# S4D convolution and gated GLU on one core: the last step's v from SBUF to SBUF, its Fourier stage ahead of two more down blocks, the last bank's skip weights on VectorE

## The chip, the cores and the metric

The kernel runs on one core of a Trainium2 chip. The metric is the device time of one execution in microseconds, the median of several executions. A core has a matrix engine (TensorE, PE in the profile), a vector engine (VectorE, DVE), a scalar engine (ScalarE, ACT), a general engine (GpSimd, POOL) and SyncE (SP), which does nothing here but issue DMAs. Each engine works through its own instructions in order. SBUF is the on-chip memory of 128 partitions, PSUM the accumulators that PE writes. 16 DMA engines move data between SBUF and device memory (DRAM) or from SBUF to SBUF. An engine that issues a DMA spends some time on the issue alone; the data lands later.

## The reference

One sequence of 2048 rows and 448 columns is normalised. On it go a long convolution (S4D: 448 channels, a kernel from 256 complex modes for each, convolved by FFT, and a skip term) and a gated unit with 1792 hidden columns. Both are added to the input.

```python
x = A_u                                   # [1, 2048, 448]
xn = _layernorm(x, axis=-1)
# A: S4D convolution
dt = exp(log_dt); A = -exp(log_A_real) + 1j * A_imag
C = (C_real + 1j * C_imag) * dt[:, None]
P = exp((A * dt[:, None])[:, :, None] * pos[None, None, :])
K = 2.0 * einsum("dn,dnl->dl", C, P).real
y = irfft(rfft(xn.T, 2 * L) * rfft(K, 2 * L), 2 * L)[:, :, :L].T
yA = y + xn * D_skip
# B: gated unit
h = sigmoid(xn @ w_gate) * (xn @ w_up)
yB = h @ w_down
return x + yA + yB
```

## The kernel before

Two streams of work are interleaved by weights: `glu()` (B) and the convolution's (A). Each is a Python generator that yields how much PE work it has just written; the driver lets the stream that is behind write next. The tile scheduler then orders the instructions of each engine by what is ready, with two helps in the code: `with hp(HP)` gives instructions a high priority, and `tc.issue_after(ins)` keeps instructions behind a given one. What was written together mostly stays together, and each engine runs its list in order.

**The convolution.** Its kernels K are built 8 channels at a time, in 56 chunks (`NCK`); four chunks fill one PSUM bank `ko` (L615), 14 banks in all. When a bank is closed (`cn % 4 == 3`), ACT copies it to SBUF (`ks<-ko`, L625), POOL adds the skip weights `dm` to its first column (`ks[:, :, 0]`, 128x8, L626), and PE runs the first Fourier stage on it (`first_stage`, into PSUM `kp` and `kq`, L565). ACT copies the result to `sk` and writes it to the DRAM tensor `sk_d`. For the last bank `first_stage` is written with high priority, at once.

Then `spectra()` goes through 17 steps `(h, k)`: half `h` of the columns and four frequency rows from `k` on. `loads` fetches a table, a part of `sk_d` (`skl`) and a part of the transformed input. `there` takes the second Fourier stage of both on PE (`sp`), copies one by ACT (`kc`) and multiplies them on DVE (`yy`, `pd`, L912 to L915). `back` takes the first inverse stage on PE (`pv`, L928), ACT copies it to SBUF (`vt`, 128x4x224, L934), and SP writes `vt` to the DRAM tensor `v_d` (L944). `turned` reads it back turned round (L950): `v_d`'s 448 KB land in 16 of the 128 partitions of `vp`, every eighth from `k // 4` on. Within `vt` partition 4w + q holds, for the four rows i of the step, what belongs to partition 32q + 8i + k/4 of `vp`, at place w. When all eight steps of a half are in `vp`, `last(h, m)` takes the last inverse stage on PE (pv from `wf` and `vp`, L961: 64 matmuls for the two calls m, m + 2) and DVE adds the result to the sums (L969): for m = 0 and 2 to `ac` (the first 1024 rows), for m = 4 and 6 to `accs[2]` and `accs[3]` (`acc` in the profile).

**The gated unit.** It takes the rows in two halves of two tiles of 512 rows. Each tile goes through gate and up matmuls (`gu`, in three passes with high and low parts of the operands), the gate on ACT and DVE (`th`, `hf` L719, `hh`, `hl` L726) and down blocks: 128 rows each, 9 matmuls into `po` (L824) and an add to `acc` on DVE (L829). In the second half some weights are loaded raw and split by POOL into `wh` (a cast, L768) and `wl` (the remainder, L769). The very last group of the unit is called `final`. For its second tile (t = 1) there are four down blocks b = 0 to 3, and the end of the program is there: the calls `lasts[0](1, m)` of the convolution's last stage are written between these blocks, and `out` (L239) writes finished rows to the output, on SP and ACT in turn.

Two more things are near these places: `bk`, a table of 128x2x128, is loaded by POOL at the start of `spectra`, and `ac` is filled from `acc_d` by four SP loads during the steps.

Of the kernel before, what the change touches and what calls it, by code (L numbers as in the profile page):

```python
# [36 lines left out]
HP = 300  # L37
# [94 lines left out]
def s4d_glu_kernel(ctx, tc, io):  # L132
# [327 lines left out]
    def kgen(pk):  # L460
# [124 lines left out]
        for g in range(NCK // NCH):  # L585
            for c in range(NCH):
                cn = g * NCH + c
                S = nxt
                me, mf = (m[:, 2 * DC * (c % 2) : 2 * DC * (c % 2) + 2 * DC] for m in mags)
                if 0 < c < 7 and NCH * (g + 1) < NCK:  # L590
                    with tc.issue_after(fts[0].ins):
                        powers(pms, g + 1, PWS[c], sins[0])
                if cn + 1 < NCK:
                    nxt = ahead(cn + 1)
                    if c % 2 == 1:
                        squares(coming[0])
                yield WK / 2
                Et = tl[f"Et{cn % 2}"]
                Ft = tl["Ft"]
                two = lambda ap: ap.unsqueeze(1).to_broadcast([128, 2, 2 * DC, 32])  # L600
                v.tensor_tensor(Et[:, :, :, 32:64], two(me[:, :, 32:64]), S[:, 1::-1], ALU.mult)  # L601
                v.tensor_tensor(Et[:, :, :, 0:32], two(me[:, :, 0:32]), S[:, 1:3, :, ::-1], ALU.mult)  # L602
                fts[:] = [v.tensor_tensor(Ft, two(mf), S[:, 3:5], ALU.mult)]  # L603
                if cn + 2 < NCK and c % 2 == 0:
                    coming = magnitudes(cn // 2 + 1)
                if c % 2 == 1:
                    mags = coming
                if cn % 4 == 0:
                    ko = psc[-1].tile([128, 8, 64], F32, name="ko", bufs=1)
                for q in range(2):  # L610
                    sl = 2 * (cn % 4) + q
                    for k in range(4):
                        h, cc = k // 2, k % 2
                        for j in range(4):
                            mm = nc.tensor.matmul(  # L615
                                ko[32 * j : 32 * j + 32, sl],
                                Ft[:, cc, DC * h + 4 * q + j],
                                Et[:, cc, DC * h + 4 * q + j],
                                start=(k == 0),
                                stop=(k == 3),  # L620
                                skip_group_check=True,
                            )
                if cn % 4 == 3:
                    ks = tl["ks"]
                    nc.scalar.copy(ks, ko)  # L625
                    nc.gpsimd.tensor_tensor(ks[:, :, 0], ks[:, :, 0], dm[:, cn // 4], ALU.add)  # L626
                yield WK / 2
                if cn % 4 == 2 and cn > 3 or cn + 1 == NCK:

                    with hp(HP) if cn + 1 == NCK else tc.issue_after(glu_mm[0].ins):  # L630
                        first_stage((cn - 3) // 4 if cn + 1 < NCK else cn // 4)
# [97 lines left out]
    def glu():  # L729
        for half in range(2):  # L730
# [4 lines left out]
            for fs_ in ORDER[half]:  # L735
# [68 lines left out]
                for t in range(2):  # L804
                    acc = accs[2 * half + t]
                    for b in range(4):
                        if final and (t, b) == (0, 1):

                            yield None
                        if final and t == 1 and b >= 2:  # L810

                            sp_mm[:] = glu_mm
                            for m in (4 * b - 8, 4 * b - 6):
                                lasts[0](1, m)
                            if b == 3:
                                out(accs[2], 8, 4, slice(H, D), (nc.sync, nc.scalar))
                                out(accs[3], 12, 3, slice(0, D), (nc.sync, nc.scalar))
                        po = psg.tile([128, D], F32, name="po", tag="gu", bufs=4)
                        bs = slice(128 * b, 128 * b + 128)
                        n = 0  # L820
                        with tc.issue_after(sp_mm[0].ins) if glu_on else nullcontext():
                            for (hh, hl), (dh, dl) in zip(hs[t], wts):
                                for a_, w_ in ((hh, dh), (hh, dl), (hl, dh)):
                                    glu_mm[:] = [nc.tensor.matmul(  # L824
                                        po, a_[:, bs], w_, start=(n == 0), stop=(n == 3 * fc - 1)
                                    )]
                                    n += 1
                        with hp(HP):
                            v.scalar_tensor_tensor(  # L829
                                acc[:, b], po, 0.5, acc[:, b], ALU.mult, ALU.add  # L830
                            )
                        yield 0.6 * fc
                        if cross and (t, b) in downs:
                            step(*downs[t, b])
                    if cross:
                        nc.sync.dma_start(acc_d[:, 4 * t : 4 * t + 4], acc)
                    if final and t == 0:
                        out(acc, 8, 4, slice(0, H), (nc.gpsimd,))
                    elif final:
                        out(acc, 15, 1, slice(0, D), (nc.sync, nc.scalar))  # L840

    def spectra(pf):
# [76 lines left out]
        def back(h, k, ys_):  # L919
            vt = work("vt", [128, 4, H], 2)  # L920
            bt, n = (t32[:, 1:3], 1) if k == 32 else (bk, 2)
            pvs = [bank("pv") for _ in range(n)]
            with after():
                for j in range(2):
                    for e in range(2):
                        for i in range(n):
                            s = slice(64 * i, 64 * i + 64)
                            mm = nc.tensor.matmul(  # L928
                                pvs[i][:, j], bt[s, e], ys_[j][s, e], start=(e == 0), stop=(e == 1),
                                skip_group_check=True,  # L930
                            )
            sp_mm[:] = [mm]
            for i in range(n):
                nc.scalar.copy(vt[:, i::2], pvs[i])  # L934


            if k == 32:
                for j in range(2):
                    nc.sync.dma_start(v_d[j, 0, 1::2, 0], vt[0:128:2, 2 * j])
            elif k == 0:  # L940
                nc.sync.dma_start(v_d[h, 0, 0::2], vt[0:128:2])
                nc.sync.dma_start(v_d[h, 0, 1::2, 1:4], vt[1:128:2, 1:4])
            else:
                nc.sync.dma_start(v_d[h, k // 4], vt)  # L944

# [65 lines left out]
            yield WS  # L1011
        sp_mm[:] = glu_mm
        back(*prev)
        for t in (*wait, prev[:2]):
            turned(*t)

    def conv():
# [136 lines left out]
```

## Time and profile before

| | |
|---|---|
| time, median of 3 runs (lowest, highest) | 715.69 us (715.16, 718.53) |
| the profiled execution's own time | 711.65 us |
| its span in the trace | 709.9 us |
| mean granted clock of PE | 0.984 |
| last matmul ends | 703.2 us |
| last add of DVE (L829) | 703.20 to 703.82 us |

The page gives one execution, taken by the hardware profiler. "Span" is the time from the first to the last instruction or landing; the execution's own time has 1.75 us more. Times in the views count from the start of the span. The chain that ended last is followed back from the last instruction: at each step to whatever released it, so a change in what is on the chain can move the end, and a change beside it moves the end only if it becomes late enough to join. "PEldq", "SPq" and "ACTq" are the engines' sequencers, which issue DMAs and wait at semaphores. Rows of groups read: line, engine, operation, output<-input, count, then the shortest, median and longest duration in ns, and when the first and the last began. Rows of single instructions begin with the start and the duration in us. Rows of windows give, for a stretch of time, the busy us of PE, PE's weight loads, DVE, ACT and POOL with the count of instructions, PE's granted clock, the DMA engines' mean share and the GB/s moved.

### The profile page before, as it was taken

Reading aid. Unit: us, or ns where it says so; the run is one execution under the profiler, and the core shown is the slowest. Engines: PE = TensorE matmul, PEld = TensorE weight load, DVE = VectorE, ACT = ScalarE, POOL = GpSimd, SP = SyncE. Lnnn points to the kernel's source line nnn. Section 1 sums busy time; section 2 is a strip of 40 time slices with the busy share of each in tenths; the row PEclk is TensorE's granted clock in tenths of the full one; section 3 lists DMA queues with packets and bytes.
Section 4 is the critical chain, followed back from the end, with each engine's and each line's share of the span. In section 5 each row is a group of like instructions: output and inputs, shape, how many; then the busy total and the mean of one; then the engine's idle time right before and its main releaser. Section 6 shows DMA issues by size and latency. Waiting matters only on the chain.

```text
span 709.9 us, 19096 instructions
## 1 busy us (share of the span) xinstructions
PE 669.7 (94%) x7752; PEld 526.9 (74%) x7752; DVE 559.8 (79%) x766; ACT 428.8 (60%) x678; POOL 386.4 (54%) x433
## 2 busy tenths in 40 slices
PE   2797999999998998999999999999989999999996
PEld 2575888778877885756878878877777777777784
DVE  5899997689999999898489899988947555565544
ACT  3655975488698779987577778778543322322320
POOL 2100137645999979896447798798755001335001
PEclk9998999999999999989999999999999999999999
DMA  9947174364244435546933333142259988899756
GB/s 199 245 145 227 52 210 160 130 209 139 69 154 155 150 81 162 186 132 203 283 103 103 92 112 112 64 146 74 56 169 284 250 236 237 222 292 251 182 151 181
DMA packets 93031, 117.22 MB, mean 165 GB/s; under 512 B 12240, under 2 KB 76624, under 8 KB 92944
## 3 DMA queue, kind: packets, MB, share of 16 engines
q1 hardware_dynamic: 65376, 91.75, 45.8%
q10 hardware_dynamic: 24896, 18.13, 8.8%
q0 software_dynamic: 2672, 6.13, 3.2%
q8 instruction: 61, 1.00, 0.6%
q14 instruction: 26, 0.21, 0.1%
HBM read 72.13 MB, written 43.84 MB: 163 GB/s over the span
## 4 chain that ended last, share of the span: by engine, by line
PE 68%; DVE 11%; DMA 7%; ACT 4%; SPq 3%; POOL 3%; issue 2%; ACTq 0%; DVEq 0%; POOLq 0%
PE gu L708 28%; PE po L824 15%; PE sp L901 7%; PE ko L615 6%; PE pv L928 4%; PE tr L541 4%; SPq L491 2%; DVE Ft L603 2%; POOL me L519 1%; DMA wraw<-in_B_w_gate_dram 1%; DVE Et L602 1%; PE pv L961 1%; DMA xe<-in_A_u_dram 1%; DVE Et L601 1%; DMA ph<-ph_d 1%
## 5 line engine op out<-in xcount | busy, mean ns | idle before, releaser
L519 POOL TENSOR_TENSOR me<-me,pm 128x32 f32<-128x32 f32 (+1 forms) x168 | 148.0, 881 | 61.5 <-DVE Et L602 34.1
L519 POOL TENSOR_TENSOR mf<-mf,pm 128x64 f32<-128x64 f32 (+1 forms) x112 | 121.3, 1083 | 5.3
L708 PE MATMUL gu<-xh,wh 128*128 128x512 f32 x336 | 100.7, 406 | 1.7 <-DVE acc L829 0.9
L708 PE MATMUL gu<-xh,wl 128*128 128x512 f32 x336 | 96.6, 391 | 0.0
L708 PE MATMUL gu<-xl,wh 128*128 128x512 f32 x336 | 95.5, 391 | 0.0
L824 PE MATMUL po<-dh,hh 128*128 128x448 f32 x224 | 85.2, 381 | 5.2 <-DVE hf L719 4.6
L601 DVE TENSOR_TENSOR Et<-me,S 128x1024 f32<-128x1024 f32 x56 | 81.8, 1462 | 10.4 <-ACT S L550 8.8
L547 ACT ACTIVATE S<-tr 128x1024 f32<-128x1024 f32 x56 | 57.8, 1032 | 47.6 <-PE tr L541 42.2
L603 DVE TENSOR_TENSOR Ft<-mf,S 128x1024 f32<-128x1024 f32 x56 | 82.3, 1469 | 4.4 <-PE ko L615 2.3
L602 DVE TENSOR_TENSOR Et<-me,S 128x1024 f32<-128x1024 f32 x56 | 81.2, 1449 | 5.0 <-ACT me L532 4.6
L824 PE MATMUL po<-dl,hh 128*128 128x448 f32 x224 | 83.3, 372 | 0.0
L824 PE MATMUL po<-dh,hl 128*128 128x448 f32 x224 | 82.0, 370 | 0.0
L724 ACT CAST hh<-hf 128x512 fp32r<-128x512 f32 x56 | 34.9, 624 | 71.8 <-DVE hf L719 66.8
L708 PEld LDWEIGHTS gu<-xh,wh 128*128 128x128 f32 x336 | 61.2, 191 | 21.6 <-issue 4.6
L708 PEld LDWEIGHTS gu<-xh,wl 128*128 128x128 f32 x336 | 62.9, 188 | 14.5 <-DVE ve L255 0.7
L615 PEld LDWEIGHTS ko<-Et,Ft 128*32 128x32 f32 x3584 | 55.4, 112 | 24.2 <-issue 12.3
L708 PEld LDWEIGHTS gu<-xl,wh 128*128 128x128 f32 x336 | 62.9, 188 | 13.5
L615 PE MATMUL ko<-Et,Ft 128*32 128x64 f32 x3584 | 66.2, 225 | 3.5 <-DVE Ft L603 3.3
L785 POOL TENSOR_TENSOR dl<-rd,dh 128x448 fp32r<-128x448 f32 x14 | 26.2, 1868 | 77.3 <-ACT dh L784 40.0
L550 ACT ACTIVATE S<-S,hpi 128x1024 f32<-128x1024 f32 x56 | 65.7, 1173 | 0.0
L719 DVE SCALAR_TENSOR_TENSOR hf<-th,gu 128x512 f32<-128x512 f32 x56 | 38.0, 679 | 34.3 <-PE gu L708 33.6
L726 DVE TENSOR_TENSOR hl<-hf,hh 128x512 fp32r<-128x512 f32 x56 | 46.7, 833 | 18.6 <-ACT hh L724 14.1
(208 smaller groups left out, 1310.7 us busy)
## 6 DMA issues: line engine op xcount, KB each, us to landing
sk_d<-sk ACTq DMA_DIRECT2D x14, 512.0 KB
sx<-x_d SPq DMA_DIRECT2D x32, 224.0 KB
skl<-sk_d SPq DMA_DIRECT2D x16, 448.0 KB
vp<-v_d SPq DMA_DIRECT2D x16, 448.0 KB
v_d<-vt SPq DMA_DIRECT2D x14, 448.0 KB
ph<-ph_d SPq DMA_DIRECT2D x224, 24.0 KB
wt_d<-wh SPq DMA_DIRECT2D x9, 512.0 KB
wt_d<-wl SPq DMA_DIRECT2D x9, 512.0 KB
```

Source lines behind the costliest of these rows:

```text
L519: ins = nc.gpsimd.tensor_tensor(m[:, :, w + a : 2 * w : n], m[:, :, a:w:n], par(base + i).unsqueeze(2).to_broadcast([128, 4 * DC, w // n]) ...
L547: nc.scalar.activation(rows(cs), pv, AF.Abs)
L550: sins[:] = [nc.scalar.activation(cs, cs, AF.Sin, scale=-TWO_PI, bias=hpi)]
L601: v.tensor_tensor(Et[:, :, :, 32:64], two(me[:, :, 32:64]), S[:, 1::-1], ALU.mult)
L602: v.tensor_tensor(Et[:, :, :, 0:32], two(me[:, :, 0:32]), S[:, 1:3, :, ::-1], ALU.mult)
L603: fts[:] = [v.tensor_tensor(Ft, two(mf), S[:, 3:5], ALU.mult)]
L615: mm = nc.tensor.matmul(ko[32 * j : 32 * j + 32, sl], Ft[:, cc, DC * h + 4 * q + j], Et[:, cc, DC * h + 4 * q + j], start=(k == 0), stop=( ...
L708: glu_mm[:] = [nc.tensor.matmul(ps, a_, b_, start=(n == 0), stop=(n == len(mm) - 1))]
L719: marks[1] = v.scalar_tensor_tensor(hf, th, 1.0, pgu[1], ALU.add, ALU.mult)
L726: v.tensor_tensor(hl, hf, hh, ALU.subtract)
L824: glu_mm[:] = [nc.tensor.matmul(po, a_[:, bs], w_, start=(n == 0), stop=(n == 3 * fc - 1))]
L901: mm = nc.tensor.matmul(to, tb[:kk, t, 64 * c : 64 * c + 64], rhs, start=True, stop=True, skip_group_check=True,)
```

## The change

Three things. For the last bank of the convolution's kernels (chunk 55), ACT copies all columns but the first, and DVE writes the first column: `ks[:, :, 0] = ko[:, :, 0] + dm`, with PSUM as one input. For the last step, (1, 28), `vt` isn't written to `v_d` and read back; 16 DMAs write it from SBUF to SBUF into `vp`, one for each of the 16 partitions of `vp`, each of 28 KB from 32 partitions of `vt`, in turn on SP, ACT, SP, ACT, POOL. And the two pairs of last-stage calls stand ahead of the down blocks b = 1 and b = 3 of the last tile, where they stood ahead of b = 2 and b = 3.

```diff
--- before.py
+++ after.py
@@ -622,8 +622,13 @@
                             )
                 if cn % 4 == 3:
                     ks = tl["ks"]
-                    nc.scalar.copy(ks, ko)
-                    nc.gpsimd.tensor_tensor(ks[:, :, 0], ks[:, :, 0], dm[:, cn // 4], ALU.add)
+                    if cn + 1 < NCK:
+                        nc.scalar.copy(ks, ko)
+                        nc.gpsimd.tensor_tensor(ks[:, :, 0], ks[:, :, 0], dm[:, cn // 4], ALU.add)
+                    else:
+                        with hp(HP):
+                            nc.scalar.copy(ks[:, :, 1:], ko[:, :, 1:])
+                            v.tensor_tensor(ks[:, :, 0], ko[:, :, 0], dm[:, cn // 4], ALU.add)
                 yield WK / 2
                 if cn % 4 == 2 and cn > 3 or cn + 1 == NCK:
 
@@ -807,10 +812,10 @@
                         if final and (t, b) == (0, 1):
 
                             yield None
-                        if final and t == 1 and b >= 2:
+                        if final and t == 1 and b in (1, 3):
 
                             sp_mm[:] = glu_mm
-                            for m in (4 * b - 8, 4 * b - 6):
+                            for m in (2 * b - 2, 2 * b):
                                 lasts[0](1, m)
                             if b == 3:
                                 out(accs[2], 8, 4, slice(H, D), (nc.sync, nc.scalar))
@@ -940,6 +945,12 @@
             elif k == 0:
                 nc.sync.dma_start(v_d[h, 0, 0::2], vt[0:128:2])
                 nc.sync.dma_start(v_d[h, 0, 1::2, 1:4], vt[1:128:2, 1:4])
+            elif (h, k) == steps[-1]:
+                engs = (nc.sync, nc.scalar, nc.sync, nc.scalar, nc.gpsimd)
+                for n in range(16):
+                    q, i = n % 4, n // 4
+                    p = 32 * q + 8 * i + k // 4
+                    engs[n % 5].dma_start(vp[h][p : p + 1], vt[q::4, i])
             else:
                 nc.sync.dma_start(v_d[h, k // 4], vt)
 
@@ -1011,7 +1022,7 @@
             yield WS
         sp_mm[:] = glu_mm
         back(*prev)
-        for t in (*wait, prev[:2]):
+        for t in wait:
             turned(*t)
 
     def conv():
```

How this moves the instructions is seen in each engine's list. DVE around the last bank, before; rows give the line, the operation, output<-input and the shape, and `yy` is the first product of the convolution's steps (the weight split `wl` of POOL isn't on this engine):

```order
L719 SCALAR_TENSOR_TENSOR hf<-th,gu 128x512
L726 TENSOR_TENSOR hl<-hf,hh 128x512
L719 SCALAR_TENSOR_TENSOR hf<-th,gu 128x512
L726 TENSOR_TENSOR hl<-hf,hh 128x512
L912 TENSOR_TENSOR yy<-kc,sp 128x448
```

And of the changed kernel, whose lines below the first edit count 5 more:

```order
L724 SCALAR_TENSOR_TENSOR hf<-th,gu 128x512
L731 TENSOR_TENSOR hl<-hf,hh 128x512
L631 TENSOR_TENSOR ks<-ko,dm 128x8
L724 SCALAR_TENSOR_TENSOR hf<-th,gu 128x512
L731 TENSOR_TENSOR hl<-hf,hh 128x512
L917 TENSOR_TENSOR yy<-kc,sp 128x448
```

The new add stands behind one `hl` of the gated unit and ahead of the next `hf`; everything else keeps its place.

DVE at the end of the program, before (`acc<-po,acc` is a down block's add, `ac<-ac,pv` and `acc<-acc,pv` are the last stage's):

```order
L915 TENSOR_TENSOR yy<-pd 128x224
L829 SCALAR_TENSOR_TENSOR acc<-po,acc 128x448 x6
L969 TENSOR_TENSOR ac<-ac,pv 128x2x224 x4
L829 SCALAR_TENSOR_TENSOR acc<-po,acc 128x448
L969 TENSOR_TENSOR acc<-acc,pv 128x2x224 x4
L829 SCALAR_TENSOR_TENSOR acc<-po,acc 128x448
```

and of the changed kernel:

```order
L920 TENSOR_TENSOR yy<-pd 128x224
L834 SCALAR_TENSOR_TENSOR acc<-po,acc 128x448 x5
L980 TENSOR_TENSOR ac<-ac,pv 128x2x224 x4
L834 SCALAR_TENSOR_TENSOR acc<-po,acc 128x448 x2
L980 TENSOR_TENSOR acc<-acc,pv 128x2x224 x4
L834 SCALAR_TENSOR_TENSOR acc<-po,acc 128x448
```

The first pair of last-stage calls moves one down block earlier, and the second keeps its place ahead of the last block; the matmuls on PE move in the same way.

SP's DMAs at the end, before (`out_dram` is the output; the two pairs of `v_d` and `vp` are those of the steps (1, 24) and (1, 28)):

```order
L944 DMA v_d<-vt 128x896
L950 DMA vp<-v_d 16x32x224
L944 DMA v_d<-vt 128x896
L950 DMA vp<-v_d 16x32x224
L239 DMA out_dram<-ac 32x4x224 x4
L239 DMA out_dram<-acc 32x4x224 x2
```

and of the changed kernel:

```order
L955 DMA v_d<-vt 128x896
L961 DMA vp<-v_d 16x32x224
L953 DMA vp<-vt 1x32x224 x7
L239 DMA out_dram<-ac 32x4x224 x4
L239 DMA out_dram<-acc 32x4x224 x2
```

SP's last write of `v_d` and last read of `vp` are gone, and 7 of the 16 direct DMAs stand there. ACT has 6 more of them, behind its two copies to `vt` and ahead of its outputs, and POOL 3, ahead of its outputs of the rows that the first tile finished. In the program the DMAs of SP and ACT take turns at eight counters that tell of their landing, and one that takes a counter again waits for the earlier one to land. So SP's last three of the seven wait for the landing of three of the first five of the 16, ACT's fourth for the landing of the `vp` read of step (1, 24), and ACT's last two for the first and the fourth of the 16. Elsewhere POOL loads `bk` ahead of the cast to `dh` that it stood behind, and SP's fourth load of `ac` stands ahead of a load of `skl` that it stood behind.

## The prediction

> **What bounds the kernel now.** I read the page first, then the chain that ended last, then PE's waits, then the two places that the change touches.
>
> ```profile
> span 709.9 us, 19096 instructions
> ...
> PE 68%; DVE 11%; DMA 7%; ACT 4%; SPq 3%; POOL 3%; issue 2%; ACTq 0%; DVEq 0%; POOLq 0%
> ```
>
> The chain runs on PE for 68% of the span. From 526 us to the last matmul PE's waits (view of waits, 526 to 712 us) have one entry, which is the wait that ends there:
>
> ```profile
> PE kp L565 <- POOL ks L626: 1.8, 1, 1.8
> ```
>
> So from 526 us on PE works without a pause that another engine ends, and whatever shifts PE there shifts the end by as much. The pieces of the chain at both places:
>
> ```profile
> 524.37 0.03 issue
> 524.40 0.90 POOL wh L768
> 525.30 0.11 issue
> 525.40 0.66 POOL ks L626
> 526.06 0.04 issue
> 526.10 0.27 PE kp L565
> ...
> 686.30 9.49 PE po L824 x45
> 695.79 1.67 PE pv L961 x64
> 697.46 2.01 PE po L824 x9
> ...
> 703.20 0.62 DVE acc L829
> ```
>
> PE stands still from 524.37 to 526.10, since the skip weights' add waits behind POOL's cast of a weight tile. At the end PE goes from one down block (po, 9 matmuls, 2.01 us) to the last Fourier stage (pv) and back; what follows the last add of 703.20 is output DMA. The change can win at three places at most: those 1.73 us, PE's work at the end (which stays the same), and the tail from 703.82 to 709.9.
>
> **VectorE adds the last bank's skip weights.** Removed: one POOL add (0.66 us, in the chain). Added: one DVE add of 128x8. The ACT copy ahead of it stays, with 63 of 64 columns.
>
> ```profile
> 524.63 0.58 ACT L625 COPY ks<-ko 128x512 f32<-128x512 f32 x1
> 524.76 1.22 DVE L726 TENSOR_TENSOR hl<-hf,hh 128x512 fp32r<-128x512 f32 x1 [0.69 <-ACT hh L724]
> 526.02 2.37 POOL L769 TENSOR_TENSOR wl<-wraw,wh 128x1024 fp32r<-128x1024 f32 x1
> L258 DVE TENSOR_TENSOR z<-ys x9: 149/161/166, 9.8 to 72.1; 128x4 f32<-128x4 f32 x6, 128x8 f32<-128x8 f32 x3
> ```
>
> The new add stands behind hl on DVE, and hl ends at 524.76 + 1.22 = 525.98: it takes 1.22 us in place of the usual 0.69, because POOL's cast (524.40 to 525.30) is in its way. So the add runs from 525.98 for 0.16 us (the 128x8 row of L258), and with the 0.04 us of the chain from one engine to the next kp starts at 526.18, where it starts at 526.10 today. The cover of the removed POOL add was hl all along: **+0.1 us, not a gain**. If the cast came after hl, hl would end at 525.45 and kp could start at 525.65: -0.45 is the lower bound. The upper one: with its add gone, POOL's wl stands straight behind the cast. If wl went ahead of hl, hl and the add behind it would wait for 2.37 us. The nearest rows, from 545 us, show the same pair cast and wl with DVE work beside it:
>
> ```profile
> 546.39 0.54 DVE L915 TENSOR_TENSOR yy<-pd 64x224 f32<-64x224 f32 x1
> 546.86 0.60 DVE L913 TENSOR_TENSOR pd<-kc,sp 64x448 f32<-64x448 f32 x1
> 547.39 2.03 DVE L914 TENSOR_TENSOR yy<-yy 64x224 f32<-64x224 f32 x1
> 545.46 1.23 POOL L768 CAST wh<-wraw 128x1024 fp32r<-128x1024 f32 x1 [6.69 <-DMA wraw<-in_B_w_up_dram]
> 546.77 2.40 POOL L769 TENSOR_TENSOR wl<-wraw,wh 128x1024 fp32r<-128x1024 f32 x1
> ```
>
> L915, asked for during the cast, came through at 546.93, ahead of wl's reading; L914, asked for after wl had begun, took 2.03 us in place of 0.38. hl is in the place of L915, so I take the good order. L913, which reads PSUM and one SBUF tile as the new add does, took its usual 0.60 beside wl. The Trainium skill's page "SBUF — State Buffer", section "Who interferes with whom", says it as a rule: a DVE instruction with two SBUF inputs contends with a GpSimd instruction that reads SBUF, one with at most one SBUF input doesn't. The trace agrees with it at L914 and L913; were the new add stopped by wl, the sum would be 2.3 us higher.
>
> On POOL the load of bk moves from behind the dh cast to ahead of it. dl, and the five weight loads behind it, then start about 0.5 us earlier (the length of that issue), so the cast of 545.46 may meet L914's first run at 545.41. PE takes its pv there off this DVE work, so up to +0.5 us, or nothing; the loads land when the DMA engines let them, and I take 0. On SP the fourth ac load goes ahead of one skl load, which is wanted a whole step later: 0.
>
> **The last stage moves ahead of block 1.** No PE work is added: the first pair of last steps starts one po block (a fifth of the chain's 9.49 us for 45 matmuls, 1.90 us) earlier than 695.72, at 693.8, and the second pair stays. What it needs is vp, and today vp is only just there:
>
> ```profile
> 695.72 1.74 PE L961 MATMUL pv<-vp,wf 64*32 64x224 f32 x64
> L961 PEldq EVENT_SEMAPHORE x9: 51/51/3042, 629.7 to 692.1; - x9
> 685.32 0.54 SPq L950 DMA_DIRECT2D vp<-v_d  x1
> 687.32 0.32 SPq L944 DMA_DIRECT2D v_d<-vt  x1
> 690.68 0.54 SPq L950 DMA_DIRECT2D vp<-v_d  x1
> ```
>
> PE's sequencer stood at this wait from 692.1 for 3.04 us, to 695.1, 0.6 us ahead of its use. With the old route the moved stage would wait 1.3 us. The new route must land 1.3 us earlier.
>
> **v from SBUF to SBUF.** Removed: the write of 687.32, the 3.36 us that SP waits for it, and the read of 690.68. Added: 16 DMAs of 28 KB, each from 32 partitions into one: 7 on SP, 6 on ACT, 3 on POOL. In the new order SP's last three and ACT's last two wait, each, for an earlier one of the same 16 to land (ACT's fourth for the vp load of 685.32), so there are two waves.
>
> ```profile
> 686.33 0.97 ACT L934 COPY vt<-pv 128x448 f32<-128x448 f32 x2 [3.89 <-PE pv L928]
> L239 ACTq DMA_DIRECT2D out_dram<-ac x4: 376/470/897, 698.5 to 700.0; - x4
> DMA to landing us min/median/max: 2.3/4.7/6.5
> 686.00:687.00 1.00, 1.00 (x8) 0.72 (x5) 0.00 (x0) 0.67 (x2) 0.00 (x0) 1.00 0.26 40
> 687.00:688.00 1.00, 1.00 (x7) 0.91 (x6) 0.00 (x0) 0.29 (x1) 0.00 (x0) 1.00 0.95 271
> 688.00:689.00 1.00, 1.00 (x6) 0.92 (x5) 0.61 (x1) 0.00 (x0) 0.00 (x0) 1.00 1.24 244
> ```
>
> The first wave is issued from 687.3 on: four on SP at 0.32 (row of v_d), three on ACT at 0.47. It queues behind the vp load of 685.32, as the write does today, and if it lands as that write does, it is there 3.36 us later, at 690.7. The second wave lands 2.3 us (the quickest of the POOL outputs, in the row of landings) to 3.36 us after that: 693.0 to 694.1, so PE waits 0 to 0.3 us; I take 0.1. POOL's three (0.55 us an issue) land within 2.3 to 4.7 us of some 688.9, by 693.6 at the latest. Behind these issues nothing stands on SP and ACT before the outputs of ac, and on POOL only outputs. This estimate holds if 28 KB into **one** partition go as fast as into many; that no row shows, and it is the far bound:
>
> ```profile
> 692.00:694.30 2.30, 2.30 (x13) 2.09 (x12) 0.96 (x2) 0.00 (x0) 1.27 (x3) 1.00 1.00 227
> 305.00:305.50 0.50, 0.50 (x46) 0.50 (x35) 0.50 (x2) 0.50 (x2) 0.42 (x2) 1.00 1.07 418
> ```
>
> The vp load fills 16 partitions at 227 GB/s with all DMA engines busy (share 1.00); a load into all 128 ran at 418. So the rate hangs on how many partitions are written at once: 14.2 GB/s each at 16. If a partition takes no more than that, one DMA needs 28.7 KB / 14.2 = 2.02 us. With all 16 side by side that is no loss; with one DMA for each of the three queues at a time it is 16 / 3 x 2.02 = 10.8 us.
>
> **The tail.** The outputs of ac are issued 1.9 us earlier and are out of the way when those of acc start at 702.19.
>
> ```profile
> 703.00:704.00 1.00, 0.16 (x1) 0.00 (x0) 0.62 (x1) 0.00 (x0) 0.00 (x0) 1.00 0.84 198
> 704.00:705.00 1.00, 0.00 (x0) 0.00 (x0) 0.00 (x0) 0.00 (x0) 0.00 (x0) 1.00 1.06 320
> ```
>
> From 704 on the DMA engines are full with acc's own outputs. Only the slice from 703 can fill better: (320 - 198) / 320 = 0.4 us at most. That slice is also the start of the new transfers, so I take -0.2.
>
> **Sum**: +0.1 + 0.1 - 0.2 = 0.0 us against the profiled execution's 711.65 us (span 709.9 and 1.75 around it). The median of the runs shown is 715.69, 4.0 above it; I put the same sum on it: **715.7 us**. Bounds of the small terms: -0.45 - 0.4 = -0.9 below, +0.5 + 0.3 + 0.1 = +0.9 above.
>
> **Rivals.**
> 1. *One partition at a time is slow* (slower). Data starts at 688.6, when the vp load of 685.32 is through (40 KB by 687, 271 more by 688, and the rest of its 448 KB at 244 GB/s). Then vp is full at 688.6 + 10.8 = 699.4 and PE, which has nothing else in order, waits 5.6 us: 721.3. With two DMAs side by side 16.2 us and a wait of 11.0: 726.7. It costs anything only from the point at which the 16 take longer than 693.8 - 688.6 = 5.2 us, that is with fewer than seven at a time. For it: each DMA writes a single partition, and neighbours in the list are issued together; the 227 against 418. Against it: three queues, and 1.8 KB of each DMA for each engine, little enough to run ahead. The Trainium skill's page "SBUF — State Buffer", section "Door 1: The DMA port swizzle", names such a mechanism: bandwidth goes by how many of 16 ports the partitions reach, with 27.6 GB/s measured for one port. By that page's figure one DMA takes 1.04 us, an estimate, and 16 in a row 16.6 us; the trace's 227 GB/s fits its 8 ports for the vp rows, and no run here shows one port alone.
> 2. *wl goes ahead of hl*: +2.3 us, 718.0.
> 3. *The second wave lands late by more than I think* (one or both of the landings at the 4.7 us median, ready at 695.4 to 696.7): 1.6 to 2.9 us, up to 718.6.
> 4. *The add really gains*, with the better tail: 714.8; faster by over 0.5% would need 3.6 us, more than all pauses the change touches on PE.
>
> **How the numbers follow.** Forecast 0.50; rival 1 0.33 (0.22 near 721, 0.11 near 727); rival 2 0.04; rival 3 0.08; rival 4 0.05. A measurement of this kernel tells some 0.5%, 3.6 us, from no change. Slower by more: rival 1 and little else, 0.34. Faster: 0.03. Same: 0.63. The range runs from 714.5 (the small terms' lower bound, with the runs' own scatter) to 723.0, past the 5.6 us case; it leaves out the 11 us case. The forecast's own range is 714.5 to 717.
>
> **What would show it.** The add right: kp's start, within 0.3 us of 1.8 us after the last ko, released by DVE; hl still at 1.2 us. The route right: no PE wait ahead of the first pv of the last stage, a gap there of 0.3 us as at the others. Rival 1: a gap of several us ahead of that pv, with a high DMA share at few GB/s from 689 us on. The tail right: from the last add to the end 6.0 to 6.1 us, today 703.82 to 709.9. It is wrong if PE waits anywhere else after 526 us, most likely at the pv of 549 us.

## The result and the profile after

| | before | changed |
|---|---|---|
| time, median (lowest, highest) | 715.42 us (714.95, 718.53), 4 runs | 722.12 us (720.94, 725.31), 4 runs |
| ratio, with its 95% interval | | 1.0105 [1.0068, 1.0142] |
| profiled execution's own time, span | 711.65, 709.9 us | 720.94, 719.2 us |
| last matmul ends | 703.2 us | 712.2 us |

The changed kernel is 1.0% slower. Its time lies in the range on record, but not where the forecast had it (715.7 us). PE's waits from 526 us on, in the changed kernel; the columns are us in total, times, longest:

```profile
PE pv L972 <- DMA vp<-vt: 6.1, 1, 6.1
PE kp L565 <- DVE ks L631: 3.2, 1, 3.2
PE pv L972 <- DVE pd L918: 0.2, 1, 0.2
```

Before there was one entry, 1.8 us at kp. Now kp waits 1.4 us longer, and the first last stage waits 6.1 us for the direct DMAs. The chain at the end of the changed kernel (start, us, what) shows them in two waves, and then a slow PE:

```profile
688.33 6.81 DMA vp<-vt
695.14 0.02 issue
695.16 4.59 DMA vp<-vt
699.75 0.52 issue
700.27 3.61 PE pv L972 x61
703.88 4.66 PE po L829 x18
708.54 1.68 PE pv L972 x64
710.21 2.03 PE po L829 x9
```

The DMA of 688.33, the sixth of the 16, takes 6.81 us to land, and the last of the 16, which SP issues only then, 4.59 (SP's last three wait for the second, the third and the sixth). Then the same 64 matmuls that take 1.68 us eight us later take 3.61 (before: 1.67), and the 18 of two down blocks take 4.66 (two times 2.01 before). Windows of the changed kernel, whose last three columns are PE's granted clock, DMA share and GB/s, show what goes with it:

```profile
694.14:698.90 4.76, 0.00 (x0) 0.00 (x0) 0.62 (x1) 0.00 (x0) 1.32 (x3) 0.99 0.54 127
698.90:700.27 1.37, 0.00 (x0) 0.03 (x1) 0.00 (x0) 0.00 (x0) 0.00 (x0) 0.50 0.00 0
700.27:703.88 3.61, 3.61 (x65) 2.30 (x65) 1.15 (x2) 0.00 (x0) 0.00 (x0) 0.50 0.02 5
703.88:708.54 4.66, 4.66 (x26) 4.00 (x33) 1.78 (x3) 0.00 (x0) 0.00 (x0) 0.81 0.60 157
```

After some 4.7 us without a matmul the granted clock falls to 0.50, and stays there into the down blocks. That costs (3.61 - 1.67) + (4.66 - 4.02) = 2.6 us on top of the wait.

The sum for the profiled executions: from the end of the last step's pv (686.30 before, 684.79 + 1.76 = 686.55 now) to the last matmul it is 16.9 us before and 25.7 now. Those 8.8 us are the 6.1 of the wait, the 2.6 of the clock and 0.1. At 686.55 the kernel is only 0.25 us late, since this execution came to kp's place 1.1 us early (PE's wait begins at 526.46 - 3.2 = 523.3 instead of 524.37); from the last add to the end of the span it is 6.3 us instead of 6.1.

The place of kp, in the timelines of DVE and POOL of the changed kernel:

```profile
522.34 0.69 DVE L724 SCALAR_TENSOR_TENSOR hf<-th,gu 128x512 f32<-128x512 f32 x1 [1.13 <-PE gu L713]
523.71 2.61 DVE L731 TENSOR_TENSOR hl<-hf,hh 128x512 fp32r<-128x512 f32 x1 [0.69 <-ACT hh L729]
526.25 0.16 DVE L631 TENSOR_TENSOR ks<-ko,dm 128x8 f32<-128x8 f32 x1
522.32 1.04 POOL L773 CAST wh<-wraw 128x1024 fp32r<-128x1024 f32 x1 [2.57 <-PE gu L713]
523.44 2.33 POOL L774 TENSOR_TENSOR wl<-wraw,wh 128x1024 fp32r<-128x1024 f32 x1
```

POOL's wl begins at 523.44, right behind the cast, and hl, asked for at 523.71, comes through only when wl is done: 2.61 us instead of 0.69. The new add stands behind it.

### The profile page after: what moved, and what is told of

Read it like the earlier page. It is cut to its first block, busy times and chain, and to the rows that moved or that the text cites. A ratio compares the mean times of both kernels' runs of the same rounds, so it can differ in the third digit from the quotient of the medians.

```text
span 719.2 us, 19122 instructions
## 1 busy us (share of the span) xinstructions
PE 671.7 (93%) x7752; PEld 527.6 (73%) x7752; DVE 560.3 (78%) x767; ACT 428.7 (60%) x678; POOL 390.8 (54%) x435
## 4 chain that ended last, share of the span: by engine, by line
PE 73%; DVE 11%; DMA 5%; ACT 4%; SPq 3%; issue 3%; ACTq 0%; DVEq 0%
PE gu L713 31%; PE po L829 15%; PE sp L906 7%; PE ko L615 6%; PE pv L933 4%; PE tr L541 4%; DVE Ft L603 2%; SPq L491 2%; DMA vp<-vt 2%; DVE Et L602 2%; DMA acc<-in_A_u_dram 1%; DVE Et L601 1%; PE pv L972 1%; PE kp L565 1%; DVE m L322 1%
## 5 line engine op out<-in xcount | busy, mean ns | idle before, releaser
L519 POOL TENSOR_TENSOR me<-me,pm 128x32 f32<-128x32 f32 (+1 forms) x168 | 153.4, 913 | 57.4 <-DVE Et L602 29.8
L601 DVE TENSOR_TENSOR Et<-me,S 128x1024 f32<-128x1024 f32 x56 | 80.7, 1443 | 10.2 <-ACT S L550 8.8
L731 DVE TENSOR_TENSOR hl<-hf,hh 128x512 fp32r<-128x512 f32 x56 | 49.8, 890 | 18.6 <-ACT hh L729 14.1
```

The costliest lines, as they stand in the source:

```text
L519: ins = nc.gpsimd.tensor_tensor(m[:, :, w + a : 2 * w : n], m[:, :, a:w:n], par(base + i).unsqueeze(2).to_broadcast([128, 4 * DC, w // n]) ...
L731: v.tensor_tensor(hl, hf, hh, ALU.subtract)
```

## The experiments

Executions of one kernel differ by several us (before: 710.2 to 718.8 over all runs), so two things are read of each run: the ratio with its interval, and, in its one profiled execution, the pieces that the change touches. The table has these for all runs, each from the waits, the chain and the timeline of that kernel; the last column is what the profile's pieces give over before (kp's wait less 1.8, plus pv's end to last matmul less 16.9), beside which the measured ratio can be held (0.1% is 0.7 us). A landing is the one that the chain shows.

| kernel | wait at kp | last v: first issue to last landing | wait ahead of the last stage | end of last back pv to last matmul | ratio [95%] | pieces, us over before |
|---|---|---|---|---|---|---|
| before | 1.8 | 7.8 | 0 | 16.9 | | |
| changed | 3.2 | 12.6 | 6.1 | 25.7 | 1.0105 [1.0068, 1.0142] | +10.2 |
| a1_ks_only | 3.2 | | 0 | 16.9 | 1.0025 [0.9996, 1.0055] | +1.4 |
| a2_move_only | 1.6 | 7.5 | 0.9 | 17.9 | 1.0016 [0.9986, 1.0046] | +0.8 |
| a3_route_only | 1.2 | 10.2 | 1.3 | 18.6 | 1.0046 [1.0016, 1.0076] | +1.1 |
| b2_ports | 3.3 | 10.0 | 2.2 (0.9 and 1.3) | 21.7 | 1.0112 [1.0063, 1.0161] | +6.3 |
| c1_spacer | 1.3 | | 0 | 16.9 | 0.9989 [0.9962, 1.0017] | -0.5 |
| c2_onewave | 1.6 | 8.6 | 1.7 | 19.1 | 1.0056 [1.0030, 1.0081] | +2.0 |
| c3_spread | 3.2 | 8.7 | none waits | 16.8 | one run, 714.01 us | +1.3 |
| c4_no_pool_out | 3.2 | 10.8 | 3.9 | 22.6 | 1.0115 [1.0077, 1.0154] | +7.1 |
| d1_all_mended | 1.3 | 9.5 | 0.8 | 18.2 | 1.0017 [0.9989, 1.0044] | +0.8 |
| d2_after_spacer | 1.3 | 11.2 | 4.4 | 23.9 | 1.0086 [1.0054, 1.0117] | +6.5 |
| d3_after_again | 3.2 | 12.7 | 6.1 | 24.6 | 1.0099 [1.0063, 1.0136] | +9.1 |

Two losses lie outside these pieces: waits of 1.2 and 1.1 us near 651 us in b2_ports and c4_no_pool_out, where a last-stage matmul of the other half waits for VectorE (0.4 us or less in the other kernels), and a low clock behind kp in three profiles, which a1_ks_only shows below.

### The three parts alone

**a1_ks_only**: before with the first part of the diff and nothing else; its core:

```diff
-                    nc.gpsimd.tensor_tensor(ks[:, :, 0], ks[:, :, 0], dm[:, cn // 4], ALU.add)
+                            v.tensor_tensor(ks[:, :, 0], ko[:, :, 0], dm[:, cn // 4], ALU.add)
```

> The kernel before with the VectorE add alone. My theory: the add costs nothing that a measurement can tell; PE's wait at kp is 1.7 to 2.4 us as hl ends when it did, and the time is within 0.5 us of before. Rival: in the changed kernel that wait was 3.2 us in place of 1.8, because hl took 2.61 us beside POOL's wl; if that is what the add brings about, hl takes 2.6 us here too and the time is 1.4 us above before.

PE's wait at kp was 3.2 us. My theory fell. DVE and POOL read as in the changed kernel:

```profile
527.48 2.61 DVE L731 TENSOR_TENSOR hl<-hf,hh 128x512 fp32r<-128x512 f32 x1 [0.68 <-ACT hh L729]
527.20 2.34 POOL L774 TENSOR_TENSOR wl<-wraw,wh 128x1024 fp32r<-128x1024 f32 x1
```

The ratio (1.8 us at its middle) fits the rival's 1.4 us, but its interval just reaches 1. The wait itself is not all. Windows of the wait and of a stretch behind it, and of the changed kernel behind the same wait:

```profile
527.04:530.23 3.19, 0.01 (x2) 0.01 (x1) 2.69 (x2) 0.89 (x2) 2.80 (x3) 1.00 0.12 48
531.68:535.10 3.42, 3.42 (x10) 2.65 (x9) 0.00 (x0) 0.88 (x2) 2.59 (x4) 0.50 0.66 195
526.46:533.28 6.82, 6.82 (x92) 5.50 (x94) 0.36 (x1) 1.73 (x3) 4.73 (x8) 1.00 0.55 156
```

Here PE runs 3.4 us at a granted clock of 0.50 behind the wait of 3.2 us, and so it does in c3_spread and d3_after_again; in the changed kernel, b2_ports and c4_no_pool_out, which waited 3.2 or 3.3 us too, it does not. From kp to the end of the last back's pv the three took 161.6 to 161.8 us, all others 159.8 to 160.9 (without the waits near 651 us), so where the low clock comes it costs about 1 us more.

**a2_move_only**: before with

```diff
-                        if final and t == 1 and b >= 2:
+                        if final and t == 1 and b in (1, 3):
-                            for m in (4 * b - 8, 4 * b - 6):
+                            for m in (2 * b - 2, 2 * b):
```

> The kernel before with the last stage's new place alone; v goes through device memory as before. My theory (the route is at fault, not the place): vp lands at about 695.1 us, the first last stage could start at 693.8, PE waits 1.3 us, and the time is 1.0 to 1.5 us above before. Rival (the place is at fault): 6 to 7 us above before, as in the changed kernel.

The first last stage waited 0.9 us, a little less than expected, with the granted clock at 1.00 throughout. The rival fell: the place alone costs about 1 us in the profile, and by the ratio 3.3 us at most.

**a3_route_only**: before with the last two parts of the diff, the 16 direct DMAs; their core:

```diff
+                    engs[n % 5].dma_start(vp[h][p : p + 1], vt[q::4, i])
-        for t in (*wait, prev[:2]):
+        for t in wait:
```

> The kernel before with the 16 direct DMAs alone, the last stage in its old place. My theory: the last of them lands at 699 to 700 us as in the changed kernel, the first last stage, due at 695.7, waits some 4 us in place of 6, and what PE then runs at a lower granted clock comes on top: 4 to 6 us above before. Rival (the place is at fault): within 0.5 us of before.

Measured 0.46% (3.3 us) over before, a little under what I expected; the wait in the profile was only 1.3 us, not some 4, since the last landing came at 697.2, not 699 to 700. That execution was the fastest of its twelve (713.83 us, median 717.71). Waits and chain of this kernel:

```profile
PE pv L967 <- DMA vp<-vt: 1.3, 1, 1.3
688.25 5.62 DMA vp<-vt
693.87 0.02 issue
693.89 3.32 DMA vp<-vt
697.21 0.03 issue
697.24 2.16 PE pv L967 x62
```

The two waves are there, shorter than in the changed kernel (6.81 and 4.59). After 1.3 us of waiting the clock is still 1.00. In the profiles move and route multiply: the pieces of the three parts alone add up to 3.3 us, those of the changed kernel to 10.2; the old place hides most of the late landing, the earlier place turns it into waiting, and the long wait is followed by the low clock. The times do not show it: by their middles the three parts alone add up to 0.87%, the changed kernel has 1.05%.

### Why wl came ahead of hl

**c1_spacer**: a1_ks_only with one more line behind VectorE's add.

```diff
+                        nc.gpsimd.tensor_tensor(dm[:, 0], ks[:, :, 1], dm[:, 1], ALU.add)
```

> The kernel before with the VectorE add, and one POOL add of 128x8 whose result nobody reads, put where the skip weights' add of POOL stood: it waits for ACT's copy of the bank, as that did, and stands between POOL's cast to wh and wl. Theory (spacer): the old POOL add kept wl from starting until hl was through; without it wl starts 0.08 us behind the cast and holds hl to its end. Then hl takes 0.7 to 1.3 us here and PE's wait at kp is 1.2 to 1.9 us in place of the 3.2 and 3.3 us of the three kernels with the VectorE add, and the time is that of before. Rival (the add's own place on VectorE costs the time): 3.2 us again.

The wait at kp was 1.3 us. DVE and POOL:

```profile
527.94 0.69 DVE L732 TENSOR_TENSOR hl<-hf,hh 128x512 fp32r<-128x512 f32 x1 [0.69 <-ACT hh L730]
528.55 0.16 DVE L631 TENSOR_TENSOR ks<-ko,dm 128x8 f32<-128x8 f32 x1
526.66 1.04 POOL L774 CAST wh<-wraw 128x1024 fp32r<-128x1024 f32 x1 [2.68 <-PE gu L714]
528.47 0.22 POOL L632 TENSOR_TENSOR dm<-ks,dm 128x8 f32<-128x8 f32 x1 [0.78 <-ACT ks L630]
528.66 2.37 POOL L775 TENSOR_TENSOR wl<-wraw,wh 128x1024 fp32r<-128x1024 f32 x1
```

The cast runs beside hf, as in the changed kernel, but POOL then waits 0.78 us for ACT's copy of the bank. In this time hl gets through in 0.69 us, and wl follows. This was what the removed add did unseen: its wait kept wl back. The rival fell. Every profile with VectorE's add and the spacer has 1.3 us at kp, and all but one without it 3.2 or 3.3; the one, c2_onewave, had the cast start 0.86 us behind hf, so that hl was asked for during the cast, as in the profile of before. The time of c1_spacer can't be told from that of before, and 1.3 us at kp is no gain either: with POOL's own add a3_route_only waited 1.2 and a2_move_only 1.6 us.

**d2_after_spacer**: the changed kernel with the same line:

```diff
+                        nc.gpsimd.tensor_tensor(dm[:, 0], ks[:, :, 1], dm[:, 1], ALU.add)
```

> The changed kernel with POOL's spacer add alone. Theory: PE's wait at kp falls from 3.2 us to 1.2 to 1.9, the wait and the low clock ahead of the last stage stay, and the time is 1 to 2 us below the changed kernel's (0.6 to 0.9% above before). Rival (the add is no part of the loss, its wait is made up later): the time of the changed kernel.

The wait at kp fell to 1.3 us as expected, and the wait (4.4 us) and the low clock at the end stayed. The time, 0.86% over before, is on the expected side of d3_after_again's 0.99%, but the intervals overlap: the profile shows the gain, the times don't.

### Why the direct DMAs land late

**b2_ports**: the changed kernel with the 16 in another order.

```diff
-                    q, i = n % 4, n // 4
+                    q, i = (0, 2, 1, 3)[n // 4], n % 4
```

> The changed kernel with the same 16 DMAs on the same queues, in another order of destinations: neighbours in the list now go to partitions 8 apart (7, 15, 23, 31, then 71 and so on) where before they were 32 apart (7, 39, 71, 103, then 15). If the pairs that are 32 apart hold each other up, the first wave lands 1.5 to 3 us earlier, the second with it, PE waits 3 to 4.5 us in place of 6.1, and the time is 1.5 to 4 us below the changed kernel's. If each DMA is slow because it fills one partition only, whichever is beside it, nothing changes: within 1 us of the changed kernel. The Trainium skill's page "SBUF — State Buffer", section "Door 1: The DMA port swizzle", has partitions 32 apart on one port and partitions 8 apart on different ones, and speaks for the first.

The time is that of the changed kernel. The waves took 5.51 and 3.22 us, less than in its profile, but a3_route_only, which has the old order, had 5.62 and 3.32. In both the vp read of step (1, 24), which the first wave queues behind, was issued well ahead of the first direct DMA (2.4 to 2.6 us, by SP's timeline); in the changed kernel only 1.5 us. So held against a3_route_only the order of the destinations made no difference, and how early the read is issued isn't all of it either (in c4_no_pool_out, below, it is 2.9 us ahead and the first wave takes 6.34). But the question stays open. Held against the changed kernel's own two profiles the waves are 1.2 to 1.5 us shorter and the wait is 2.2 us, even less than the first expectation asked; the interval of the ratio leaves room for 2.5 us below the changed kernel; and in the new order neighbours also read the same 32 partitions of vt, where they read different ones. What the Trainium skill's page "SBUF — State Buffer", section "Door 1: The DMA port swizzle", says of partitions 32 apart sharing a port is neither borne out nor refuted by this.

**c4_no_pool_out**: the changed kernel without the line

```diff
-                        out(acc, 8, 4, slice(0, H), (nc.gpsimd,))
```

> The changed kernel without POOL's four outputs of the first tile's rows (rows 1024 to 1535, the first 224 columns are not written), which move 448 KB from 694.5 to 697.5 us, when the second wave lies on the DMA engines. If they hold the second wave up: it lands 2.5 to 3 us after the first in place of 4.6, PE waits 4.0 to 4.6 us in place of 6.1, and the time falls by 1.5 to 2 us. Rival: the second wave takes 3.2 us or more all the same (3.3 and 3.2 us in the two other kernels with the route), and what was long in the changed kernel was the vp read of step (1, 24) ahead of it.

The second wave took 3.19 us with these transfers gone, as it took 3.32 and 3.22 with them in a3_route_only and b2_ports, and the first took 6.34. The time did not fall, but its interval would hide 1.5 us; PE's wait was 3.9 us, as short as the first expectation has it. So POOL's outputs are not the main cause, and a part for them stays open. In the changed kernel and d3_after_again, which had the long second waves (4.59 and 4.43 us), POOL issued its first output ahead of the three DMAs of SP's second wave (693.24 against 693.98 us, 699.38 against 700.35); in a3_route_only and b2_ports two of the three were issued ahead of it.

**c3_spread**: the same DMAs into another tile (`v2`, a vt buffer); the extra read that its expectation names is left out of the diff.

```diff
-                    p = 32 * q + 8 * i + k // 4
-                    engs[n % 5].dma_start(vp[h][p : p + 1], vt[q::4, i])
+                v2 = work("vt", [128, 4, H], 2)
...
+                    engs[n % 5].dma_start(v2[32 * q : 32 * q + 32, i], vt[q::4, i])
```

> The changed kernel's 16 DMAs in their order and on their queues, from the same 32 partitions and with the same packets of 896 bytes, but each fills 32 partitions of a free vt buffer at one place, where it filled 32 places of one partition of vp. vp's rows of the last step hold an older step's v in place of it, read once more at step (1, 0), so the last stage does not wait for these DMAs. What counts is their time to landing. If a single partition as destination is slow: 2.3 to 4 us to landing at the median, in place of 6.5 and 5.0, and packets of 40 to 90 ns throughout, where they took up to 270. Rival (it is the number of small DMAs and packets, or what else is on the queues): the median to landing stays at 5 to 6.5 us.

This is best held against d3_after_again, in which the vp read ahead of the DMAs landed as long behind the first copy to vt (some 4.3 us in both). SP's row spans its issues from the first to the end of the last, which waits for a landing of the first wave; the windows (last column GB/s) start 1.9 us behind the first issue on SP in c3_spread and 1.8 us behind it in d3_after_again:

```profile
689.13 6.57 SPq L953 DMA_DIRECT2D vt<-vt  x7
691.00:692.00 1.00, 1.00 (x7) 0.91 (x6) 0.26 (x1) 0.00 (x0) 0.06 (x1) 1.00 1.12 253
692.00:693.00 1.00, 1.00 (x7) 0.90 (x6) 0.51 (x1) 0.00 (x0) 0.00 (x0) 1.00 1.13 192
693.00:694.00 1.00, 1.00 (x7) 0.91 (x6) 0.12 (x1) 0.00 (x0) 0.00 (x0) 1.00 0.34 82
```

```profile
693.24 9.11 SPq L953 DMA_DIRECT2D vp<-vt  x7
695.00:696.00 1.00, 1.00 (x7) 0.91 (x6) 0.36 (x1) 0.00 (x0) 0.16 (x1) 1.00 1.24 151
696.00:697.00 1.00, 1.00 (x6) 0.92 (x5) 0.41 (x1) 0.00 (x0) 0.00 (x0) 1.00 1.16 61
697.00:698.00 1.00, 1.00 (x6) 0.91 (x5) 0.22 (x1) 0.00 (x0) 0.00 (x0) 1.00 1.00 62
698.00:699.00 1.00, 1.00 (x7) 0.91 (x6) 0.55 (x1) 0.00 (x0) 0.00 (x0) 1.00 0.26 38
```

With one partition as destination the DMA engines are as busy (share 1.00 to 1.16) at 61 to 62 GB/s: each packet holds its engine longer; what it waits for no row shows. With 32 partitions the same stretch moves 192 and 82 GB/s and is over. By the packet records those of 896 bytes, the read's last ones among them, took 74 ns at the median and at most 120 in c3_spread (691.5 to 693.6 us); in the changed kernel it was 254 ns, and up to 356 (690.0 to 691.5 us). In the changed kernel's second wave, with fewer of these DMAs under way, the median was 41 ns again: single partitions are slow here where many such DMAs run at once. From the first issue to the last landing it is 8.7 against 12.7 us. The time to landing that the view gives is that of POOL's three DMAs: 4.1/4.3/4.4 us (least, median, most), against 5.2/6.5/6.7; I had asked for 2.3 to 4 us, so a good part of the time to landing is not the single partition, but the read ahead. Counted from the landing of that read, by the landings in the traces, all 16 were through after 4.5 us in c3_spread. Into single partitions it took 6.9 to 8.3 us in two waves (six profiles) and 5.6 and 6.3 us in one (c2_onewave, below, and d1_all_mended). So of what comes behind the read the single partitions cost the most, 2.4 us or more, and the second wave some 0.6 to 2.7.

**c2_onewave**: the changed kernel with

```diff
-                engs = (nc.sync, nc.scalar, nc.sync, nc.scalar, nc.gpsimd)
+                engs = (nc.sync, nc.scalar, nc.gpsimd, nc.gpsimd)
-                    engs[n % 5].dma_start(vp[h][p : p + 1], vt[q::4, i])
+                    engs[n % 4].dma_start(vp[h][p : p + 1], vt[q::4, i])
```

> The changed kernel with the same 16 DMAs dealt out in turn to SP, ACT, POOL, POOL: four each on SP and ACT and eight on POOL, so that none waits for another of the 16 to land. Theory (two waves): the second wave cost 3.2 to 4.6 us in all three kernels with the route; without it the last landing is 4 to 7 us behind the first copy to vt, at most 1.5 us after POOL's last issue (8 issues of 0.55 us), PE's wait ahead of the last stage falls from 6.1 us to 0 to 2.5 us, and the granted clock stays at 1.00. The time is 4 to 6 us below the changed kernel's. Rival (the DMAs are slow in total, whatever the waves): the last landing comes 10 us or more after the copy to vt, and PE waits 4 us or more.

PE's wait and the chain of this kernel:

```profile
PE pv L972 <- DMA vp<-vt: 1.7, 1, 1.7
687.72 5.60 DMA vp<-v_d
693.32 0.02 issue
693.34 5.19 DMA vp<-vt
698.53 0.14 issue
698.67 2.31 PE pv L972 x59
```

The wait is within what I expected, the clock stays at 1.00, and the time is 3.5 us below the changed kernel's (0.56% over before against 1.05%; the intervals overlap a little, and in the profile 1.6 us of the gain are at kp, where the cast came late). But the last landing is 8.6 us behind the first issue on SP, more than the 4 to 7 I gave it: one wave is better than two and still slower than the way by device memory (7.8 us).

**d3_after_again**: the changed kernel unaltered.

> The changed kernel once more, beside the same runs of before: 1.0% above before. What is asked is whether its profiled execution was a usual one: by the theory PE's wait ahead of the last stage is over 3.4 us again, with the granted clock at 0.5 behind it, and the wait at kp 3.2 us.

It came out as expected: kp 3.2 us, the last stage 6.1 us, the waves 7.05 and 4.43 us, the granted clock at 0.50 from 703 us on. In these the first profile was a usual one.

### Everything mended

**d1_all_mended**: the changed kernel with the spacer's line, c2_onewave's two lines and the old place:

```diff
+                        nc.gpsimd.tensor_tensor(dm[:, 0], ks[:, :, 1], dm[:, 1], ALU.add)
+                engs = (nc.sync, nc.scalar, nc.gpsimd, nc.gpsimd)
-                        if final and t == 1 and b in (1, 3):
+                        if final and t == 1 and b >= 2:
```

> The changed kernel with POOL's spacer add ahead of wl, the 16 DMAs in one wave (four on SP, four on ACT, eight on POOL) and the last stage back in its old place. Theory: of the three losses (wl ahead of hl, the second wave, a use 1.9 us earlier) none is left, but nothing is won either: the last landing comes 8.5 to 9 us behind the first copy to vt, against 7.85 us by device memory with 0.6 us to spare, so PE waits 0 to 1 us ahead of the last stage and 1.2 to 1.9 us at kp, and the time is that of before to 0.3% or less. Rival (the direct route gains once it is in one wave): no wait ahead of the last stage and 0.5 us or more below before.

As the theory had it: 1.3 us at kp, 0.8 us ahead of the last stage, 9.5 us for v (a little over my 8.5 to 9), and a time that can't be told from before. The direct route gains nothing here even so. None of the versions beats before by what these runs can tell; c1_spacer comes nearest, at 0.9989 [0.9962, 1.0017].

## Why the prediction was right and wrong

- **What bounds the kernel** held: from 526 us to the end, what PE waits is what the kernel loses, and what the low clock behind a wait adds. The pieces of the profiles agree with the ratios within their intervals, but for the changed kernel's first profile, c2_onewave's and a3_route_only's, which lie at the edge (10.2 us against 4.9 to 10.1, 2.0 against 2.1 to 5.8, 1.1 against 1.1 to 5.4).
- **VectorE's add**: the step that failed is "the cover of the removed POOL add was hl all along: +0.1 us". The term was +1.4 us, and about 1 us more where the low clock followed. I took it that hl would come ahead of wl because L915, asked for during the cast, did; but that order hung on when the cast starts. The case was among the rivals (2, at 2.3 us), with a chance of 0.04. c1_spacer shows what I had not seen: the removed add did two things, and holding wl back was the one that mattered.
- **The move** held in its mechanism and size: with the old route 0.9 us of waiting where I gave 1.3.
- **The route**: the step that failed is "if it lands as that write does, it is there 3.36 us later" for the first wave, and 2.3 to 3.36 us for the second. Measured: 6.81 and 4.59 us (7.05 and 4.43 in the second profile), so the term for PE's wait was 6.1 us instead of 0.1. That two waves come, I had right, from the list of instructions. Rival 1 had the time (vp full at 699.4 us, a wait of 5.6 us, 721.3 us in all; measured 699.75, 6.1 and 722.1), in part by luck, since it priced neither kp nor the clock, and the right sign of its mechanism: single partitions do hold the packets up (c3_spread). But not as it priced it, one DMA after another all the way: part is the second wave (c2_onewave), and the read ahead is late itself: beside the direct DMAs it took 5.5 to 6.3 us to land (4.9 in c3_spread, 4.5 before). The range held only because it was drawn past this rival; the forecast's own mechanism did not hold.
- **The clock** was in no step. Ahead of the last stage a wait of 3.9 to 6.1 us (changed, c4_no_pool_out, d2, d3) was followed by a granted clock of 0.50 at the next matmuls, a single wait of 1.7 us or less (a2, a3, c2, d1) was not; but in b2_ports two waits of 0.9 and 1.3 us, with 1.0 us of matmuls between them, were, and the 3.2 us at kp were in three profiles of six. So the length of one wait does not decide it alone. The Trainium skill's page "TensorE: Matmul & The Clock Gate", section "Part 1: The HAM clock gate (the "warmup" mystery)", puts that at one idle window of about 3.4 us. These runs show it after less. The low clock adds 2.6 us at the end of the changed kernel, and a rival with a long wait should have had it in its price.
- **The tail**: -0.2 us forecast, +0.2 in the profile. Neither matters.

The forecast's chance of "no change" rested on two estimates that were each taken at the good end. What stays open: how the loss on the route divides exactly between the single partition, the second wave, the read ahead and POOL's outputs. Each was changed alone in one kernel at most, and they overlap. That the low clock comes from idleness was read from runs with longer and shorter waits; no run kept PE busy through the same wait.

## What to carry to other kernels

An instruction that is taken off an engine may have been the only thing that held back the next one on it: look at what that one disturbs when it starts earlier. A way that skips device memory isn't shorter if it needs many small DMAs into single partitions, least of all if the counters force them into two waves; count the waves, and give a transfer that has never been seen in the trace the price of the slowest case. Where a moved use may wait 2 to 3 us or more, add the price of matmuls at half the clock behind it: here it came after 2.2 us in two pieces, and in three cases of six after 3.2 us.

## What had not been expected of the hardware

- DMA engines can be full (share 1.00 to 1.16) at 61 GB/s when most destinations are single partitions of SBUF (d3_after_again, 696 us), where 418 GB/s went into all 128 (before, 305 us).
- In the changed kernel's second wave the DMA engines moved their last bytes at some 697.5 us, and the landing came at 699.75. The vp read of before landed 0.85 us behind its last bytes (694.3, 695.15).
- VectorE's add of 128x8 with one input in PSUM took 0.16 us also while wl ran (c2_onewave, 528.49 us, wl from 528.11 on); hl, with two inputs in SBUF, took 2.61 in the changed kernel. The Trainium skill's page "SBUF — State Buffer", section "Who interferes with whom", says that a DVE instruction with at most one SBUF input, outside the 2-port modes, does not contend with GpSimd, and one with two does while GpSimd reads SBUF. The traces agree.
